# Attention, experts and a gated layer in one kernel: which queue loads the first batch's values of the strided heads

## The chip, the cores and the metric

The kernel runs on one core of one Trainium2 chip. The metric is the device time of one launch in microseconds (us). The engines are named as the profile names them: PE (TensorE, the matrix engine; PEld is its weight load), DVE (VectorE), ACT (ScalarE), POOL (GpSimd) and SP (SyncE). SP computes nothing here: its in-order queue issues nearly all transfers between HBM and the on-chip memory. POOL can issue transfers too, on a queue of its own, and computes besides.

## The reference, cut to what matters

Three stages follow one another; the output of one is the input of the next.

```python
# attention: 4 batches, 8 heads, 576 positions, head size 64
mask_local   = (rel >= 0) & (rel < 32)
mask_strided = (rel >= 0) & (pos[None, :] % 32 == pos[:, None] % 32)
masks = [mask_local for heads 0..3, mask_strided for heads 4..7]
scores = where(masks, q @ k.T / 8, -1e9);  attn = softmax(scores) @ v
# 2304 tokens x 512: noisy top-2 routing over 8 experts, relu(x @ w1) @ w2 each
# then rmsnorm, silu(xn @ w_gate) * (xn @ w_val) @ w_out
```

For a strided head, position `32*i + r` sees only the positions `32*i' + r` with `i' <= i`. So its scores fall apart into 32 residues `r` of 18 positions each, and the kernel treats six or seven residues together as one block of 108 or 126 rows.

## The kernel before, in words

The program is written out by hand in the order in which every engine is to run it; nothing reorders it afterwards. An engine's queue is in order, so an instruction that waits holds up all that stand behind it on that engine.

The attention is one loop over 40 units: for each batch `b` and kind (`"L"` local, heads 0 to 3; `"S"` strided, heads 4 to 7) five units `j`. The order is (0,L), (0,S), (1,S), (1,L), (2,S), (2,L), (3,S), (3,L). Pass `i` of the loop (lines 733 to 785) issues the scores of unit `i`, the transposes of the probabilities of unit `i-1`, the product with the values of unit `i-2` (`pv`, line 473) and the store of the result of unit `i-3` to the buffer `xd` in HBM (`store_x`, line 494). Beside its own scores a pass transposes queries and keys of the *next* group of units on PE (`t_unit`, line 336, whose transposes are line 344): during passes 3 and 4 those of (0,S), during passes 5 to 9 those of (1,S).

Three loaders feed this.

- `load_nat(b, kind)` (line 196, issue on line 205) brings queries and keys of four heads as they lie in HBM: eight loads of 128 positions each, key and query alternating (`natk`, `natq`), and two of the last 64 positions (`natr`). Every row that is moved is 256 bytes. All ten go through SP's queue.
- `load_vl(b)` (line 226) brings the values of the local heads in five loads through SP's queue.
- `load_vs(b, g)` (line 219, issue on line 222) brings the values of the strided heads for block `g` of residues (`vs0` to `vs4`), one load for each of four heads: 126 rows for the first two blocks, 108 for the other three, 256 bytes a row. These go through POOL's queue. For the first batch all twenty are issued at the start (lines 255 and 256); for later batches four at a time, in the loop, once `pv` has used the block before.

The program opens with the ten loads of (0,L), the five of the local values and the ten of (0,S) on SP (lines 238 to 240), while POOL sets constants and zero patches and then issues the twenty loads of `vs` for batch 0. On pass 3 `routing_consts` (line 312) adds three more loads to SP (`wgn` twice and `nz`) and some constants to POOL, and the first `store_x` follows. On pass 4 come the ten loads of (1,S).

The instructions that matter below are thus, on SP: line 205 (queries and keys), line 222 (strided values), lines 313, 314 and 316 (routing inputs), line 504 (results to `xd`); on PE: line 344 (transposes of queries and keys), line 480 (product with the strided values); on DVE: line 357 (the copy of the transposed strided keys to `ks`).

Of the kernel before, what the change touches and what calls it, by code (L numbers as in the profile page):

```python
# [24 lines left out]
def attn_moe_swiglu(ctx: ExitStack, tc: tile.TileContext, q, k, v, w_gate, w_noise, noise, w1, w2,  # L25
                    u_gate, u_val, u_out, rms_g, out):
    nc = tc.nc
    B, H, S, D = q.shape
# [18 lines left out]
    NI = S // WIN  # L47
# [148 lines left out]
    def load_nat(b, kind, parts=range(5)):  # L196

        h0 = 0 if kind == "L" else 4
        for a in parts:
            for nm, src in (("k", k), ("q", q)):  # L200
                n, o, m = (128, 0, 4) if a < 4 else (64, 0 if nm == "q" else 64, 1)
                key = (nm if a < 4 else "r", b, kind)
                if key not in nat:
                    nat[key] = ap_.tile([128, m, 256], F32, name="nat" + key[0], bufs=2)
                nc.sync.dma_start(nat[key][o:o + n, a % 4].rearrange("p (h d) -> p h d", d=D),
                                  bass.AP(tensor=src.tensor,
                                          offset=src.offset + ((b * H + h0) * S + a * 128) * D,
                                          ap=[[D, n], [S * D, 4], [1, D]]))

    vs_t = [ap_.tile([128, 4, D + 1], F32, name=f"vs{g}") for g in range(5)]  # L210
# [5 lines left out]
    qs2 = [[ap_.tile([128, S], F32, name=f"qs{i}{j}") for i in range(2)] for j in range(2)]  # L216
    ks2 = [[ap_.tile([128, S], F32, name=f"ks{i}{j}") for i in range(2)] for j in range(2)]

    def load_vs(b, g):
        r0, nr = GR[g]  # L220
        for h in range(4):
            nc.gpsimd.dma_start(vs_t[g][:nr * NI, h, 0:D],
                              bass.AP(tensor=v.tensor, offset=v.offset + ((b * H + 4 + h) * S + r0) * D,
                                      ap=[[D, nr], [WIN * D, NI], [1, D]]))

    def load_vl(b, parts=((0, 9),)):
        for t0, t1 in parts:
            if t0 == 0:
                nc.sync.dma_start(vl[32:96, 0, :, 0:D],
                                  bass.AP(tensor=v.tensor, offset=v.offset + b * H * S * D,  # L230
                                          ap=[[D, 64], [S * D, 4], [1, D]]))
                t0 = 1
            for h in range(4 if t1 > 1 else 0):
                nc.sync.dma_start(vl[:96, t0:t1, h, 0:D],
                                  bass.AP(tensor=v.tensor, offset=v.offset + ((b * H + h) * S + 64 * t0 - 32) * D,
                                          ap=[[D, 96], [64 * D, t1 - t0], [1, D]]))

    load_nat(0, "L", (0, 1, 2, 3, 4))
    load_vl(0)
    load_nat(0, "S")  # L240


    dif = ap_.tile([128, 128], F32, name="dif")
# [8 lines left out]
    nc.gpsimd.memset(vl[0:32, 0, :, 0:D], 0.0)  # L252
    for t in vs_t:
        nc.gpsimd.memset(t[:, :, D:D + 1], 1.0)
    for g in range(5):
        load_vs(0, g)
    identb = ap_.tile([128, 128], BF, name="identb")
    V.tensor_copy(identb, identf)
    mapf = ap_.tile([128, E * NT], F32, name="mapf")
# [473 lines left out]
    for i in range(NS + 3):  # L733
        u = subs[i] if i < NS else None
        if u:
            b, kd, j = u
# [25 lines left out]
        if 0 <= i - 2 < NS:  # L762
            w = subs[i - 2]
            pv(w)
            if w[0] + 1 < B:
                if w[1] == "S":
                    load_vs(w[0] + 1, w[2])
                elif w[2] == 4:
                    load_vl(w[0] + 1)
# [680 lines left out]
```

## Time and profile before

| what | value |
|---|---|
| median of 3 runs | 1095.3 us (1095.11 to 1097.02) |
| the profiled execution's own time | 1100.19 us |
| its span, first to last instruction | 1098.4 us |
| PE busy | 1051.4 us, 96% of the span |
| DVE, ACT, POOL busy | 700.1, 494.5, 223.1 us |
| moved by DMA | 196.13 MB, mean 179 GB/s |
| mean granted clock of TensorE | 0.982 of full |

The profile is of one execution, which took 0.4% longer than the median of the runs. Busy shares are averages over stages with different limits: the attention takes about the first 200 us and is a tightly coupled stage in which every engine waits for others, and the experts and the gated layer after it keep PE busy throughout. The stage of the change is the first 60 us.

### The profile page before, as it was taken

How to read it: one execution, taken by the hardware profiler on the slowest of the kernel's cores; microseconds unless marked ns; L12 is line 12 of the kernel's file. 1: busy time of each engine (PE TensorE's matmuls, PEld its weight loads, DVE VectorE, ACT ScalarE, POOL GpSimd, SP SyncE). 2: the span in 40 equal slices, each digit the busy share in tenths (PEclk: the TensorE clock that was granted, in tenths of full speed). 3: DMA queues.
4: the chain of work that ended last, by engine and by line, in shares of the span. 5: the costliest groups of instructions: out<-in, count | busy, mean ns of one | idle time of the engine just before them, and what ended most of it. 6: DMA issues, size and time to landing. Idle time of an engine off the chain costs nothing. (4 is left out here: it accounts for less than half of the span.)

```text
span 1098.4 us, 17694 instructions
## 1 busy us (share of the span) xinstructions
PE 1051.4 (96%) x6309; PEld 944.9 (86%) x6309; DVE 700.1 (64%) x1489; ACT 494.5 (45%) x1044; POOL 223.1 (20%) x261
## 2 busy tenths in 40 slices
PE   7988989999999999999999999999999999999998
PEld 5776777889989999999898989888999888999997
DVE  4666665457788788876354144878876566754554
ACT  4766652353443444443344144545454554543342
POOL 6565210303232323222200034111000220000000
PEclk8989889999999999999999999999999999999999
DMA  9977522358798898775444133455456554464431
GB/s 162 206 177 162 129 62 64 96 176 267 267 300 279 284 287 296 261 246 184 164 155 143 48 115 98 146 203 174 168 201 231 195 175 148 159 216 166 140 135 58
DMA packets 179418, 196.13 MB, mean 179 GB/s; under 512 B 66816, under 2 KB 135424, under 8 KB 179328
## 3 DMA queue, kind: packets, MB, share of 16 engines
q1 hardware_dynamic: 169264, 172.37, 49.8%
q0 software_dynamic: 9920, 22.35, 7.7%
q8 instruction: 50, 0.82, 0.3%
q14 instruction: 40, 0.33, 0.1%
q10 hardware_dynamic: 144, 0.26, 0.1%
HBM read 140.88 MB, written 54.00 MB: 177 GB/s over the span
## 5 line engine op out<-in xcount | busy, mean ns | idle before, releaser
L149 PE MATMUL bank<-xta,low 128*128 128x384 f32 x376 | 128.0, 340 | 3.1 <-DVE posu L956 2.0
L151 PE MATMUL bank<-xta,low 128*128 128x384 f32 x376 | 127.9, 340 | 0.0
L150 PE MATMUL bank<-xta,low 128*128 128x384 f32 x376 | 127.7, 340 | 0.0
L149 PE MATMUL bank<-ring,ha 128*128 128x512 f32 x288 | 114.3, 397 | 0.0
L150 PE MATMUL bank<-ring,ha 128*128 128x512 f32 x288 | 114.0, 396 | 0.0
L151 PE MATMUL bank<-ring,ha 128*128 128x512 f32 x288 | 114.0, 396 | 0.0
L149 PE MATMUL bank<-low 128*128 128x384 f32 x264 | 89.8, 340 | 7.3 <-ACT p L1294 7.2
L150 PE MATMUL bank<-low 128*128 128x384 f32 x264 | 89.7, 340 | 0.0
L151 PE MATMUL bank<-low 128*128 128x384 f32 x264 | 89.5, 339 | 0.0
L1030 POOL TENSOR_TENSOR dm<-dm,da 128x512 f32<-128x512 f32 x36 | 46.7, 1296 | 203.7 <-DVE da L1028 101.8
L162 ACT ACTIVATE ha<-bank 128x384 fp32r<-128x384 f32 x64 | 31.4, 490 | 116.5 <-PE bank L151 116.4
L149 PEld LDWEIGHTS bank<-xta,low 128*128 128x128 f32 x376 | 71.3, 190 | 11.4 <-issue 3.3
L163 DVE SCALAR_TENSOR_TENSOR ha<-bank,ha 128x384 fp32r<-128x384 f32 x64 | 35.4, 553 | 63.4 <-ACT ha L162 63.3
L150 PEld LDWEIGHTS bank<-xta,low 128*128 128x128 f32 x376 | 71.2, 189 | 4.9
L151 PEld LDWEIGHTS bank<-xta,low 128*128 128x128 f32 x376 | 71.2, 189 | 0.0
L846 POOL DMA_INDIRECT buf<-yd,posu x36 | 38.5, 1069 | 155.2 <-DMA yd<-buf 98.6
L1325 ACT ACTIVATE u<-u 128x384 f32<-128x384 f32 x32 | 16.8, 526 | 115.7 <-DVE u L1324 115.7
L151 PEld LDWEIGHTS bank<-ring,ha 128*128 128x128 f32 x288 | 54.0, 187 | 12.4 <-DVE ha L1127 0.3
L149 PEld LDWEIGHTS bank<-low 128*128 128x128 f32 x264 | 49.6, 188 | 15.7 <-ACT p L1294 9.8
L132 DVE TENSOR_TENSOR low<-stage,low 128x1024 fp32r<-128x1024 f32 x34 | 42.6, 1256 | 23.2 <-ACT low L131 21.4
L830 POOL DMA_INDIRECT buf<-xd,mapu x37 | 47.8, 1291 | 46.7 <-DVE posu L956 16.6
L149 PEld LDWEIGHTS bank<-ring,ha 128*128 128x128 f32 x288 | 54.1, 188 | 3.1 <-ACT ha L1125 0.3
(284 smaller groups left out, 2780.9 us busy)
## 6 DMA issues: line engine op xcount, KB each, us to landing
stage<-in_moe_w_dram SPq DMA_DIRECT2D x128, 256.0 KB
low<-ul SPq DMA_DIRECT2D x20, 896.0 KB
ul<-low SPq DMA_DIRECT2D x12, 896.0 KB
yd<-buf SPq DMA_DIRECT2D x40, 256.0 KB
ud<-dm SPq DMA_DIRECT2D x36, 256.0 KB
stage<-uc SPq DMA_DIRECT2D x16, 512.0 KB
wc<-uc SPq DMA_DIRECT2D x16, 512.0 KB
yd<-zero SPq DMA_DIRECT2D x28, 256.0 KB
```

What stands on the lines that cost most here:

```text
L132: lo_engine.tensor_tensor(r[:, 1], st, r[:, 0].bitcast(F32), op=OP.subtract)
L149: nc.tensor.matmul(o, l[(slice(None), 0) + lsl], r[(slice(None), 0) + rsl], start=first, stop=False)
L150: nc.tensor.matmul(o, l[(slice(None), 0) + lsl], r[(slice(None), 1) + rsl], start=False, stop=False)
L151: nc.tensor.matmul(o, l[(slice(None), 1) + lsl], r[(slice(None), 0) + rsl], start=False, stop=last)
L162: nc.scalar.activation(h[:, 0], p, AF.Relu)
L163: nc.vector.scalar_tensor_tensor(h[:, 1], p, 0.0, h[:, 0].bitcast(F32), op0=OP.max, op1=OP.subtract)
L830: nc.gpsimd.indirect_dma_start(t, None, xd, bass.IndirectOffsetOnAxis(ap=mapu[:, e * NT + j:e * NT + j + 1], axis=0))
L846: nc.gpsimd.indirect_dma_start(y, None, yd, bass.IndirectOffsetOnAxis(ap=posu[:, kk, t:t + 1], axis=0))
L1030: nc.gpsimd.tensor_tensor(m, m, a.bitcast(F32), op=OP.add)
L1325: nc.scalar.activation(u3, u3, AF.Silu)
```

## The change: which queue issues twenty loads, and where in it

`load_vs` gets the issuing engine as an argument. The twenty loads of batch 0 leave POOL's queue and stand in SP's queue behind the ten loads of the strided queries and keys. Later batches are loaded by POOL as before. What is loaded, the tiles, and every instruction of PE, DVE and ACT are the same.

```diff
-    def load_vs(b, g):
+    def load_vs(b, g, eng=nc.gpsimd):
         r0, nr = GR[g]
         for h in range(4):
-            nc.gpsimd.dma_start(vs_t[g][:nr * NI, h, 0:D],
+            eng.dma_start(vs_t[g][:nr * NI, h, 0:D],
                               bass.AP(tensor=v.tensor, offset=v.offset + ((b * H + 4 + h) * S + r0) * D,
                                       ap=[[D, nr], [WIN * D, NI], [1, D]]))
...
     load_nat(0, "L", (0, 1, 2, 3, 4))
     load_vl(0)
     load_nat(0, "S")
+    for g in range(5):
+        load_vs(0, g, nc.sync)
...
     for t in vs_t:
         nc.gpsimd.memset(t[:, :, D:D + 1], 1.0)
-    for g in range(5):
-        load_vs(0, g)
```

On SP's queue before, from the last load of (0,S) to the keys of (1,S) (`natk_413`; `xd` is the results' buffer, `x_340` the first unit's result):

```order
L205 DMA natr_159<-in_q_dram 64x4x64
L313 DMA wgn_217<-in_moe_w_gate_dram 128x4x8
L314 DMA wgn_217<-in_moe_w_noise_dram 128x4x8
L316 DMA nz_219<-in_moe_noise_dram 128x18x8
L504 DMA xd_62<-x_340 128x256
L205 DMA natk_413<-in_k_dram 128x4x64
```

And in the changed kernel, at the same place:

```order
L205 DMA natr<-in_q_dram 64x4x64
L222 DMA vs_115<-in_v_dram 126x1x64 x4
L222 DMA vs_116<-in_v_dram 126x1x64 x4
L222 DMA vs_117<-in_v_dram 108x1x64 x4
L222 DMA vs_118<-in_v_dram 108x1x64 x4
L222 DMA vs_119<-in_v_dram 108x1x64 x4
L313 DMA wgn<-in_moe_w_gate_dram 128x4x8
L314 DMA wgn<-in_moe_w_noise_dram 128x4x8
L316 DMA nz<-in_moe_noise_dram 128x18x8
L504 DMA xd<-x 128x256
L205 DMA natk<-in_k_dram 128x4x64
```

The twenty loads now stand between the keys and queries of (0,S) and everything that SP issued behind them: the routing inputs, the first result's store and the ten loads of (1,S).

On PE the order is unchanged. This is the piece of it in which the keys of (1,S) are first used; what PE does next, products and transposes of units that are already under way, stands behind them:

```order
L416 MATMUL bank0_101<-ks10_128,qs10_124 126x126
L470 MATMUL bank3_104<-identf_67,pp_437 96x128 x2
L344 MATMUL bank5_106<-identf_67,natk_413 128x128 x4
L484 MATMUL bank4_105<-vl_120,pts_431 64x65 x8
L515 MATMUL bank6_107<-identf_67,x_465 128x128 x2
```

These four transposes read all four 128-position loads of keys, the last of which is the seventh of the ten loads on SP. Nothing moved here.

## Rows read from the trace of the kernel before

**Rows 1.** The page: busy time of PE, and the granted clock in 40 slices

```profile
PE 1051.4 (96%) x6309; PEld 944.9 (86%) x6309; DVE 700.1 (64%) x1489; ACT 494.5 (45%) x1044; POOL 223.1 (20%) x261
PEclk8989889999999999999999999999999999999999
```

**Rows 2.** Timeline of PE: start us, us, engine, line, op, out<-in, count [idle before <-releaser]

```profile
3.24 0.66 PE L385 MATMUL bank<-identf,natk 128*128 128x128 f32 x2 [3.24 <-DMA natk<-in_k_dram]
...
21.86 0.48 PE L344 MATMUL bank<-identf,natk 128*128 128x128 f32 x1 [1.99 <-DMA natk<-in_k_dram]
22.12 1.06 PE L344 MATMUL bank<-identf,natq 128*128 128x128 f32 x4
23.11 1.14 PE L484 MATMUL bank<-vl,pts 96*64 96x65 f32 x16
...
31.34 0.60 PE L344 MATMUL bank<-identf,natk 128*128 128x128 f32 x4
31.88 0.69 PE L484 MATMUL bank<-vl,pts 96*64 96x65 f32 x16
...
37.59 0.99 PE L480 MATMUL bank<-vs,pts 126*126 126x65 f32 x8
```

**Rows 3.** Windows: stretch, its us, busy us of each engine (instructions), granted clock, DMA share, GB/s

```profile
9.64:19.20 9.56, 7.61 (x61) 6.50 (x60) 5.75 (x27) 6.77 (x24) 8.16 (x15) 1.00 1.33 181
16.88:21.86 4.98, 0.94 (x6) 0.33 (x4) 0.45 (x3) 2.38 (x9) 2.99 (x13) 0.99 1.34 186
21.86:28.90 7.04, 6.61 (x41) 5.66 (x41) 3.36 (x6) 2.97 (x6) 0.00 (x0) 0.52 1.03 139
...
31.30:45.80 14.50, 14.15 (x148) 11.88 (x147) 9.73 (x30) 11.37 (x34) 6.92 (x12) 1.00 0.97 197
```

**Rows 4.** Timeline of POOL: the twenty loads (two rows of four) and what follows

```profile
5.44 8.11 POOL L222 DMA_DIRECT2D vs<-in_v_dram  x13
...
17.35 1.80 POOL L222 DMA_DIRECT2D vs<-in_v_dram  x3 [0.40 <-DMA vs<-in_v_dram]
19.11 0.19 POOL L315 MEMSET wgn<- 128x64 f32 x1
```

**Rows 5.** DMA issues over all four batches: out<-in, queue, count, KB each

```profile
vs<-in_v_dram POOLq DMA_DIRECT2D x48, 27.0 KB
...
vs<-in_v_dram POOLq DMA_DIRECT2D x32, 31.5 KB
```

**Rows 6.** Timeline of SP's queue: start us, us of issue, line, out<-in, count

```profile
0.73 0.45 SPq L205 DMA_DIRECT2D natk<-in_k_dram  x1
...
9.64 1.20 SPq L205 DMA_DIRECT2D natk<-in_k_dram  x1
...
15.64 1.26 SPq L205 DMA_DIRECT2D natk<-in_k_dram  x1
...
18.59 0.61 SPq L205 DMA_DIRECT2D natr<-in_q_dram  x1
19.25 0.60 SPq L313 DMA_DIRECT2D wgn<-in_moe_w_gate_dram  x1
...
21.26 2.38 SPq L504 DMA_DIRECT2D xd<-x  x1
...
26.18 0.51 SPq L205 DMA_DIRECT2D natq<-in_q_dram  x1
...
27.83 0.51 SPq L205 DMA_DIRECT2D natk<-in_k_dram  x1
...
30.34 1.02 SPq L504 DMA_DIRECT2D xd<-x  x2
...
56.10 1.62 SPq L504 DMA_DIRECT2D xd<-x  x2
```

**Rows 7.** Waits of SP's queue in the first 60 us: who waited for whom, us, times, longest

```profile
SPq L504 <- DVE ks L357: 2.3, 1, 2.3
```

## The prediction

> **What bounds the kernel now.** The page comes first: PE is busy for 1051.4 of 1098.4 us, and the few slices with a lower granted clock lie in the first fifth [rows 1]. A change at the start therefore costs or gains what it moves PE's first stretch by; nothing behind it has idle time to take that up. Next the timeline of PE at the start: the last 128-position load of the strided keys of batch 0 arrives only at 21.86 us, and PE is held for it [rows 2]. [...] Third, SP's timeline: it issues without a pause, one transfer after the other, and the keys of (1,S), issued last at 27.83 us, are used by PE at 31.34 us without a wait but with little to spare [rows 2, 6]. [...]
>
> **What the change takes away.** POOL issues the twenty loads from 5.44 to 19.15 us [rows 4], beside SP's loads. Per batch they are 12 of 27.0 KB and 8 of 31.5 KB [rows 5], 576 KB or 0.59 MB; at the 181 to 186 GB/s of that stretch [rows 3] that is 3.2 us of the transfers' time. With them gone the last strided keys should land 3.2 us earlier, at 18.7 us, and SP, whose ten loads end at 18.59 + 0.61 = 19.20 us [rows 6], at 16.0 us. The bounds: nothing, if the second queue used time that SP's loads could not; and 4.1 us, if the ten loads, which took 9.64 to 19.20 us or 0.96 each, fell to the 0.55 of a quiet stretch (26.18 to 27.83 us, three steps) [rows 6]. I take 3.2, the one that follows from bytes. POOL is free 13.7 us earlier; the constants behind its loads [rows 4] hold nobody up, so that is worth nothing. The first wait of SP's queue also goes: the first store of a result stood from 21.26 us for 2.38 us, 2.3 of it behind the copy to `ks` on DVE [rows 6, 7], which follows those keys. In the new list SP arrives there long after that copy.
>
> **What it adds.** Twenty issues on SP, ahead of the routing inputs, the first store and the ten loads of (1,S). No row has this load on SP. The nearest have the same shape, residues by 18 positions, in the other direction: two stores of strided results take 1.62 us together, 0.81 each with the gap [rows 6]. The stores of local results, one row a partition, take 1.02 for two, 0.51 each, and the quiet loads 0.55 [rows 6]. So a load costs 0.55 to 0.81 us of SP's time and all twenty 11.0 to 16.2 us. I take 0.81, by the shape.
>
> [...]
>
> SP's list is then: 16.0, plus 16.2 for the twenty, is 32.2 us; the three routing inputs took 19.25 to 21.26 us, so 34.2; the store without its wait 0.6, so 34.8; the fourth load of keys of (1,S) is the seventh of its ten, 7 times 0.55, so 38.65 us. From the end of issue to use it was 2.1 us with empty queues (0.73 + 0.45 to 3.24 us), 5.0 in the crowded stretch (15.64 + 1.26 to 21.86), and at most 3.4 for these same keys before (28.34 to the fourth transpose at 31.7) [rows 2, 6]. With SP alone issuing I take 2.5: 41.1 us. PE's queue is in order, so all that stands behind these transposes, and with it ACT and DVE, waits. Before, the fourth transpose ran at 31.7 us: **9.4 us later**.
>
> **The clock.** PE would reach that place about 25 us (31.34 less the 3.2 and less the slow stretch's loss, below) and stand for some 15 us, three times the pause after which the clock fell before. So I count one slow stretch like that from 21.86 to 28.90 us behind it. Four transposes took 1.06 us there against 0.60 later, sixteen products 1.14 against 0.69 [rows 2]; at that ratio of about 0.6, 7.04 us lose **2.8 us**. The old slow stretch goes, but its gain only lengthens the new wait. Bounds: 0, if other work hides it, to 4.8, if it lasts 12 us.
>
> **What is hidden.** The values themselves land by about 34 us, and their first use, at 37.59 us before [rows 2], stands behind the stalled transposes, so they hold nobody. The next ten loads of SP, (1,L), and everything later move with SP by about as much as PE moves, so I expect no second stall and nothing given back.
>
> **Sum:** 9.4 + 2.8 = 12.2 us. The profiled execution's 1100.2 us would become 1112.4; the median of the runs, 4.9 us below it, 1095.3 + 12.2 = **1107.5 us**. A difference of 0.2% (2.2 us) is about what a measurement of this kernel can tell from no change.
>
> **The rivals.**
> - *The loads cost SP only what any load does*, 0.55 us. Then the twenty take 11.0 instead of 16.2, the stall shrinks by 5.2, and the sum is 7.0: 1102.3 us. For it: other shapes cost that. Against it: every strided store is dearer.
> - *Nothing is gained at the start.* If POOL's transfers ran in time that SP's could not use, the keys of (0,S) still land at 21.86 and SP's list starts at 19.2: 3.2 us more, 1110.7 us. The DMA share of 1.34 against 0.97 later [rows 3] speaks for a real queue and so against it.
> - *Not slower: the transfers, not SP's issuing, set when the keys land.* Then the moved bytes only change places. Last strided keys at 18.7; the rest of (0,S), 0.26 MB, until 20.1; the values' 3.2 until 23.3; routing inputs 2.0, store 0.6, seven loads 3.85 give 29.7 us instead of 31.7: 2.0 us faster, 1093.3 us. It decides where a load costs SP little: with p per load the keys land at 16.0 + 20p + 2.0 + 0.6 + 3.85 + 2.5, which is 31.7 at p = 0.34 us, below the shortest issue in these rows, 0.45. Against it also: 31.5 KB are 0.17 us of transfer at 186 GB/s, a fifth of the issue. [...]
>
> **How the numbers follow.** Forecast 0.62, cheap loads 0.20, no gain at the start 0.12, not slower 0.06. The range must reach down to the cheap loads (1102.3) and a part of the clock's loss less, 1100.5; up to no gain at the start with a landing slower by a microsecond, 1112.0. Left out are the not-slower case and the tails. Only that case is not slower by over 0.2%: its 2.0 us lie within the 2.2, so most of it counts as no change. Faster 0.02, the same 0.05, slower 0.93.
>
> **What would show it.** Right: no wait of PE for keys beyond some 19 us; twenty rows of line 222 on SP of about 0.8 us each from 16 to 32 us; a wait of PE on `natk` of some 15 us, ended near 41 us; a granted clock near 0.5 for about 7 us after it; the first product with `vs` near 49 us instead of 37.59; from there the same distances as before. Wrong: issues well under 0.5 us, a stall that ends before 32 us, or a first expert stage that starts when it did.

## The result, and the profile after

| | before | changed |
|---|---|---|
| median, us | 1095.67 (1095.11 to 1097.02, 4 runs) | 1108.47 (1107.86 to 1109.59, 4 runs) |
| ratio, with 95% interval | | 1.0103 (1.0084 to 1.0122) |
| the profiled execution: own time, span, us | 1100.19, 1098.4 | 1108.92, 1107.1 |

The change costs 12.8 us by the medians and 11.3 by the ratio (9.2 to 13.4); 12.2 were forecast. The page after: PE is busy for as long as before to within half a per cent [rows 1], in a longer span, and the second slice, 28 to 55 us, has a lower granted clock.

```profile
PE 1046.4 (95%) x6309; PEld 940.5 (85%) x6309; DVE 701.5 (63%) x1489; ACT 494.2 (45%) x1044; POOL 210.3 (19%) x241
...
PEclk9698889999999999999999999999999999999999
```

SP's timeline after (start us, us of issue, line, out<-in, count), beside [rows 6]:

```profile
16.02 0.62 SPq L205 DMA_DIRECT2D natr<-in_q_dram  x1
16.68 15.89 SPq L222 DMA_DIRECT2D vs<-in_v_dram  x20
32.62 0.46 SPq L313 DMA_DIRECT2D wgn<-in_moe_w_gate_dram  x1
...
34.29 1.14 SPq L504 DMA_DIRECT2D xd<-x  x1
35.53 0.38 SPq L205 DMA_DIRECT2D natk<-in_k_dram  x1
...
38.77 0.51 SPq L205 DMA_DIRECT2D natk<-in_k_dram  x1
```

The loads of (0,S) end at 16.64 us instead of 19.20; the twenty new ones take 0.79 us each, and the fourth keys of (1,S) are issued at 38.77 instead of 27.83. PE's timeline after, beside [rows 2]:

```profile
18.13 0.33 PE L344 MATMUL bank<-identf,natk 128*128 128x128 f32 x1 [0.88 <-DMA natk<-in_k_dram]
...
38.56 0.48 PE L344 MATMUL bank<-identf,natk 128*128 128x128 f32 x1 [12.91 <-DMA natk<-in_k_dram]
...
42.25 0.47 PE L344 MATMUL bank<-identf,natk 128*128 128x128 f32 x1 [0.80 <-DMA natk<-in_k_dram]
...
50.36 0.99 PE L480 MATMUL bank<-vs,pts 126*126 126x65 f32 x8
```

The strided keys of batch 0 are complete at 18.13 instead of 21.86 us: the start did gain. Then PE waits 12.91 us for the first keys of (1,S), and three times more for the others, to 42.25 us; before, the four ran from 31.34 us without a wait. (In a second profile of the kernel before, below, they ran from 31.62 us, and the fourth waited 0.26 us, to 32.37.) PE's waits for keys in the first 60 us, as the view of waits adds them up (us in total, times, longest), beside 3.1 us at the very start:

```profile
PE bank L344 <- DMA natk<-in_k_dram: 16.1, 5, 12.9
```

The windows after (columns as in [rows 3]) show the wait and what it leaves behind:

```profile
17.00:25.20 8.20, 6.26 (x73) 4.89 (x71) 4.72 (x13) 6.46 (x18) 0.00 (x0) 1.00 0.38 70
25.20:36.00 10.80, 0.45 (x4) 0.17 (x2) 0.75 (x2) 1.39 (x5) 0.00 (x0) 0.59 0.25 36
36.00:43.00 7.00, 2.18 (x10) 1.08 (x12) 0.17 (x1) 0.00 (x0) 0.00 (x0) 0.50 1.07 214
43.00:48.00 5.00, 5.00 (x41) 4.08 (x38) 2.35 (x6) 1.33 (x4) 0.00 (x0) 0.54 0.98 215
48.00:56.00 8.00, 8.00 (x83) 6.97 (x82) 5.25 (x16) 6.65 (x19) 4.81 (x8) 1.00 0.96 173
```

While SP issues the twenty, the DMA share is 0.38, then 0.25: the transfers are idle for most of the time in which everything waits for SP to issue. PE stands and the granted clock falls (0.59 from 25.2 to 36 us, 0.50 from 36 to 43); from 43 to 48 us PE is busy throughout at 0.54, and from 48 us on the clock is full again (1.00). What stands behind the four transposes on PE comes after them: the next products start at 42.66 us, DVE waits 16.8 us for the four to copy them to `ks`, and ACT 17.4 us for transposes behind them.

**From there nothing is given back.** Against a second profile of the kernel before (first experiment) the same instructions of DVE come 12.0 us later at 44 to 72 us, about 13 us later at 81 us, and 13.3 us later at the end. Against the first profile of before the shift is 12.8 us at 47 to 83 us and 8.8 at the end, since that execution lost some 4.5 us by itself later, 2.9 of them between 150 and 190 us.

### The profile page after: what moved, and what is told of

The parts are those of the page before. It is cut to its first block, busy times and chain, and to the rows that moved or that the text cites. A ratio compares the mean times of both kernels' runs of the same rounds, so it can differ in the third digit from the quotient of the medians.

```text
span 1107.1 us, 17694 instructions
## 1 busy us (share of the span) xinstructions
PE 1046.4 (95%) x6309; PEld 940.5 (85%) x6309; DVE 701.5 (63%) x1489; ACT 494.2 (45%) x1044; POOL 210.3 (19%) x241
## 5 line engine op out<-in xcount | busy, mean ns | idle before, releaser
L1325 ACT ACTIVATE u<-u 128x384 f32<-128x384 f32 x32 | 16.8, 526 | 115.8 <-DVE u L1324 115.8
```

The source lines that it names most:

```text
L1325: nc.scalar.activation(u3, u3, AF.Silu)
```

## The experiments

Each run is set against runs of the kernel before in the same comparison; their medians were 1096.34 us (first four experiments, 7 runs), 1099.66 (next four, 21 runs), 1097.18 (the three after them, 23 runs) and 1100.66 (the last, 3 runs). Absolute times are not compared between comparisons: the first four ran on one chip, the next four and the last on a second, the three between on a third. On the second chip the kernel before is some 3 us slower, and all five kernels profiled there fall 2.6 to 3.1 us further behind between 150 and 190 us; no profile of the other two chips changes by more than 0.4 us there. "Shift" is how much later the same instruction of DVE comes than in the second profile of the kernel before.

### The kernel before, once more

> The kernel before, unchanged, for a second profile of it. The two profiles so far differ by 12.8 us from 60 to 140 us but only by 8.8 us at the end, while the medians differ by 12.8 us. If the profiled execution of before lost about 4 us to itself around 160 to 185 us (its granted clock is 0.83 there), a second profile is some 4 us shorter (span near 1094 us) and runs parallel to the changed kernel at a distance of 12 to 13 us to the end. If the changed kernel really regains 4 us there, the second profile looks like the first (span near 1098 us).

One execution: 1095.62 us, span 1093.8, mean granted clock 0.989. The first profile was an execution 4.6 us longer. Up to 72 us the two lie within 0.8 us of each other; in the window 150 to 200 us the granted clock was 0.95 in the first and 0.99 in this one. So the 8.8 us that the change seems to cost at the end of the first pair of profiles are the full 12 to 13 us.

### What makes a load dear: two kinds of plain rows

Both kernels load rows that lie together in HBM, in place of residues by 18 positions; the first takes 128 rows for every load, the second as many rows as the real load.

```diff
+            if eng is nc.sync:
+                eng.dma_start(vs_t[g][:n, h, 0:D],
+                              bass.AP(tensor=v.tensor, offset=v.offset + ((b * H + 4 + h) * S + r0) * D,
+                                      ap=[[D, n], [1, D]]))    # n = 128, or nr * NI = 126 and 108
+                continue
```

> The changed kernel, but the twenty loads read 128 rows that lie together in HBM instead of residues by 18 positions, so the first batch's strided heads get other values than the reference's. Theory (SP's own time per load ahead of the keys of (1,S) sets the stall, and the shape makes it dear): a load costs 0.55 instead of 0.80 us, the block on SP 11 instead of 15.9 us, the fourth transpose of the keys of (1,S) runs near 37.3 instead of 42.25 us, the kernel is about 5 us faster than the changed one, near 1103.5 us. Rival (any load on SP costs the same): 1108.5 us. Rival (bytes set it): 1108.5 us, since no byte is saved.

> As the run with 128 plain rows, but 126 and 108 rows as in the changed kernel, still lying together, so again with other values. It tells the walk (7 or 6 by 18) from the number of rows. If the walk in three steps makes a load dear: 0.55 us each and near 1103.5 us, like 128 rows. If a row count that 16 engines cannot share evenly makes it dear: 0.75 us each and near 1108 us, like the changed kernel.

SP's timeline and PE's, 128 rows:

```profile
16.58 10.76 SPq L223 DMA_DIRECT2D vs<-in_v_dram  x20
```
```profile
36.96 0.47 PE L349 MATMUL bank<-identf,natk 128*128 128x128 f32 x1 [0.74 <-DMA natk<-in_k_dram]
...
45.27 0.99 PE L485 MATMUL bank<-vs,pts 126*126 126x65 f32 x8
```

And SP's timeline with 126 and 108 rows:

```profile
16.93 10.25 SPq L223 DMA_DIRECT2D vs<-in_v_dram  x20
```

The twenty issues one by one (shortest, median and longest in ns, first and last start in us), in the changed kernel, with 128 rows, and with 126 and 108:

```profile
L222 SPq DMA_DIRECT2D vs<-in_v_dram x20: 732/732/958, 16.7 to 31.8; - x20
```
```profile
L223 SPq DMA_DIRECT2D vs<-in_v_dram x20: 429/430/1512, 16.6 to 26.9; - x20
```
```profile
L223 SPq DMA_DIRECT2D vs<-in_v_dram x20: 340/372/1638, 16.9 to 26.8; - x20
```

128 rows: 1105.41 us (4 runs), ratio 1.0087 (1.0070 to 1.0103), 9.1 us slower. 126 and 108 rows: 1103.15 us (4 runs), ratio 1.0066 (1.0049 to 1.0083), 6.8 us slower. On average a load of plain rows takes 0.54 and 0.51 us of SP, one by residues and positions 0.79, with the same bytes in the second case. The averages of the plain rows contain one issue of 1.5 and 1.6 us that was held up by something the profile does not name; the usual issue took 0.43 us for 128 rows, 0.39 for 126 and 0.37 for 108, against 0.75 and 0.73 for 126 and 108 rows by residues. So it is not the odd number of rows that makes the issue dear but the pattern, 7 or 6 residues by 18 positions. The price reaches the end: the twenty issues are 5.1 us shorter with 128 rows, the fourth transpose comes 5.3 us earlier (36.96 against 42.25), the first product with the strided values 5.1 us earlier, and the shift at 43 to 63 us is 6.9 with 128 rows and 7.6 with 126, in place of 12.0. The gain over the changed kernel is 3.7 us with 128 rows and 6.0 with 126 by the medians, 1.8 and 4.1 by the ratios, with intervals some 4 us wide: in the total a gain is clear for 126 rows alone, and its size of some 5 us is read from the profiles.

### The dose: eight loads on SP, twelve on POOL

```diff
-    for g in range(5):
+    for g in range(2):
         load_vs(0, g, nc.sync)
...
+    for g in range(2, 5):
+        load_vs(0, g)
```

> Eight of the twenty loads (the first two blocks) on SP behind the keys and queries, the other twelve on POOL from the start as before. Theory (each load ahead of the keys of (1,S) costs SP 0.79 us): the block takes 6.3 instead of 15.9 us; the strided keys come 1.8 us later than in the changed kernel, because twelve loads still run beside them (0.33 MB at 184 GB/s); the fourth transpose of the keys of (1,S) runs near 42.25 - 9.5 + 1.8 = 34.5 us, 2.8 us later than before, the clock still falls: about 5 us slower than before, near 1101 us. Rival (a fixed price as soon as SP carries such loads): near 1108 us. Rival (only transfers count): not slower than before.

SP's timeline, then PE's:

```profile
19.90 6.57 SPq L222 DMA_DIRECT2D vs<-in_v_dram  x8
```
```profile
21.40 0.33 PE L346 MATMUL bank<-identf,natk 128*128 128x128 f32 x1 [0.89 <-DMA natr<-in_q_dram]
...
32.68 0.48 PE L346 MATMUL bank<-identf,natk 128*128 128x128 f32 x1 [2.69 <-DMA natk<-in_k_dram]
...
36.30 0.48 PE L346 MATMUL bank<-identf,natk 128*128 128x128 f32 x1 [0.76 <-DMA natk<-in_k_dram]
...
44.66 0.99 PE L482 MATMUL bank<-vs,pts 126*126 126x65 f32 x8
```

1107.05 us (4 runs) against 1099.66, ratio 1.0070 (1.0047 to 1.0093), 7.4 us slower: some 2 us more than expected. It is no fixed price that comes with the first such load: the keys below are 4.6 us late, with twenty loads 10.6. With twelve loads still on POOL the start gains only half a microsecond (21.40 against 21.86). SP's eight issues add 6.6 us ahead of the keys of (1,S); the first store behind them takes 1.2 us less than before, from its start to the next (it no longer waits [rows 7]), and the seven loads up to the fourth keys 0.9 less. The fourth transpose is 4.6 us later than in the first profile of before, 3.9 later than in the second. But the short stall brings the slow stretch too (the sixteen products behind the four transposes take 1.14 us, as in the changed kernel at a granted 0.50 to 0.54, against 0.69 at this place before [rows 2]): from the fourth transpose to the first product with the strided values 8.4 us, like the 8.1 after the long one (8.3 and 9.0 with the plain rows) and unlike the 5.9 before. **Here a clock that has fallen costs about the same behind a short wait as behind a long one** (2.69 and 12.91 us), which was missing from the expectation.

### The clock behind the stall: filling it

Extra transposes of a constant, whose results are overwritten, keep PE busy ahead of the four transposes: 78 and three times 6, then, since that left a gap, 118 and three times 8.

```diff
             for a in range(4):
+                if (b, kind, u) == (1, "S", 1):
+                    for _ in range(6 if a else 78):    # second kernel: 8 and 118
+                        nc.tensor.transpose(p[:, a * 128:(a + 1) * 128], identf, identf)
                 nc.tensor.transpose(p[:, a * 128:(a + 1) * 128],
```

> The changed kernel with 78 extra transposes of the identity on PE ahead of the first transpose of the keys of (1,S), and 6 ahead of each of the other three, into a bank that the real ones overwrite. They fill the stall and change no wait. Theory (the half clock after the stall is a term of its own, 2.8 us in the prediction): the clock stays at full, the rows behind the stall take 0.60 instead of 1.06 us, and the kernel is 2.3 to 2.8 us faster than the changed one, near 1106.0 us. Rival (the slow stretch is hidden by other waits): no change, 1108.5 us. If the fillers themselves delay PE, the stall's end moves and shows it.

PE's timeline with 78:

```profile
25.22 8.68 PE L346 MATMUL bank<-identf 128*128 128x128 f32 x78
...
38.84 0.47 PE L347 MATMUL bank<-identf,natk 128*128 128x128 f32 x1 [4.95 <-DMA natk<-in_k_dram]
...
43.37 0.34 PE L347 MATMUL bank<-identf,natk 128*128 128x128 f32 x1
...
49.35 0.99 PE L483 MATMUL bank<-vs,pts 126*126 126x65 f32 x8
```

1108.55 us (4 runs), ratio 1.0113 (1.0095 to 1.0132): nothing gained. The extra transposes ran out after 8.7 us, PE stood for 4.95 us and the clock fell (0.55 from 36 to 43 us); the sixes then ran at that clock and held up the real transposes by 1.1 us. Still the clock was back by then (0.95 from 43 to 48 us), and the first product came 1.0 us earlier than in the changed kernel. So this kernel does not show what the clock alone is worth, and the next one fills for longer.

> The changed kernel with 118 extra transposes of a constant on PE ahead of the first transpose of the keys of (1,S), and 8 ahead of each of the other three; what they write is overwritten. At 0.11 us each at full clock they should fill the wait from 25.2 us to the landing at 38.6 us, and most of the three steps of 1.2 us behind it. The list of SP and the landings are as in the changed kernel. Theory (the slow clock behind the stall is worth some 2.1 to 2.3 us, the stall itself is SP's list): the granted clock stays at 1.00 up to the fourth transpose, which comes at 42.3 us as in the changed kernel, the first product with the strided values at 48.2 instead of 50.4 us, and the ratio to the kernel before falls from 1.010 to about 1.008 (9 to 11 us slower than before). Rival (the clock is worth nothing, since DVE and ACT set that stretch): the first product stays near 50.4 us and the ratio at 1.010 or more.

PE's timeline with 118, and the windows 100 to 150 and 150 to 200 us:

```profile
25.21 13.04 PE L346 MATMUL bank<-identf 128*128 128x128 f32 x118
...
42.26 0.33 PE L347 MATMUL bank<-identf,natk 128*128 128x128 f32 x1
...
48.23 0.99 PE L483 MATMUL bank<-vs,pts 126*126 126x65 f32 x8
```
```profile
100.00:150.00 50.00, 42.81 (x432) 35.37 (x431) 33.38 (x125) 32.48 (x95) 21.41 (x24) 0.93 0.65 147
150.00:200.00 50.00, 44.03 (x378) 37.92 (x379) 30.31 (x143) 20.40 (x61) 3.05 (x3) 0.97 0.20 59
```

The profile is as the theory has it: full clock throughout (1.00 from 25 to 56 us), the fourth transpose where it was, the first product at 48.23 us instead of 50.36, shift 9.9 instead of 12.0. The stall itself does not move by being filled: it is SP's list. But the times do not follow: 1109.21 us (1104.63 to 1113.56, 6 runs), ratio 1.0116 (1.0092 to 1.0140). The profiled execution was the fastest of the six. The same kernel once more:

> The same kernel as in the run with 118 and 8 extra transposes, looked at once more, because its executions lay between 1104.6 and 1113.6 us with mean granted clocks between 0.986 and 0.994, and the profiled one was the fastest of them, with 0.994. Theory (the extra transposes do save the two microseconds behind the stall in every execution, and what the others lose, they lose at a later place by another fall of the clock): the first product with the strided values comes at 48.2 us again, and an execution of 1108 to 1112 us has a stretch after 60 us in which the granted clock is lower than in the other profile and PE takes 4 to 8 us longer. Rival (the extra transposes do not always hold the clock): in such an execution the granted clock falls before 50 us and the first product comes at 50 us or later.

```profile
48.42 0.99 PE L483 MATMUL bank<-vs,pts 126*126 126x65 f32 x8
```
```profile
100.00:150.00 50.00, 43.23 (x421) 35.96 (x418) 31.56 (x117) 32.20 (x92) 20.59 (x25) 0.90 0.66 147
150.00:200.00 50.00, 42.74 (x359) 36.16 (x359) 28.21 (x136) 20.87 (x66) 4.10 (x4) 0.90 0.21 61
```

This execution took 1114.46 us, 9.8 us more than the other. Up to 63 us the two agree to 0.5 us, the first product at 48.42; then this one falls behind, to 6.3 us between 115 and 190 us, where its granted clock is 0.90 in both windows against 0.93 and 0.97, and by another 3.5 us up to 560 us. From 120 to 130 us, where it loses 1.7 us, PE is busy for all 10 us at a granted clock of 0.63, against 7.96 us at 0.99 in the other. Not all of this belongs to the kernel: the execution ran on the second chip, on which the kernel before is 3.5 us slower (1100.66 against 1097.18), and some 3 us of the loss lie between 150 and 190 us, where every kernel profiled on that chip loses them. So **the slow stretch behind the stall is worth 2.1 us where it lies, and in the times they are not to be found**: the eight executions are 12.0 and 12.5 us slower than before in the medians, the changed kernel 12.8, and the six on one chip lie 8.9 us apart. Whether the filled kernel loses more there than the changed one, and why, is open.

### Behind the next keys instead of ahead of them

The twenty loads stay on SP but stand behind the ten of (1,S).

```diff
-    for g in range(5):
-        load_vs(0, g, nc.sync)
...
                 load_nat(*units[i // 5 + 2])
+                if i == 4:
+                    for g in range(5):
+                        load_vs(0, g, nc.sync)
```

> All twenty loads on SP, but behind the ten loads of (1,S) instead of ahead of them. Theory (SP's list has no room in its first 60 us, so 16 us of issue stall somebody wherever they stand): the keys of (1,S) arrive near 27 us and that stall goes, but what stands behind the loads now, the stores of the next results and the loads of (1,L), is 16 us late, the result buffers run out near 36 us, and PE is held until about 43 us: a later, shorter stall; 1095 to 1101 us. Rival (only the place ahead of the keys of (1,S) was wrong): about 4.5 us faster than before, near 1091 us.

SP's timeline, PE's and DVE's:

```profile
27.13 15.90 SPq L222 DMA_DIRECT2D vs<-in_v_dram  x20
43.14 0.87 SPq L502 DMA_DIRECT2D xd<-x  x2
```
```profile
28.26 0.33 PE L342 MATMUL bank<-identf,natk 128*128 128x128 f32 x1 [0.90 <-DMA natk<-in_k_dram]
...
45.68 1.68 PE L478 MATMUL bank<-vs,pts 108*108 108x65 f32 x8 [4.40 <-issue]
```
```profile
45.15 0.42 DVE L490 TENSOR_TENSOR x<-bank,rc 126x256 f32<-126x256 f32 x1 [5.24 <-DMA xd<-x]
...
58.40 0.42 DVE L490 TENSOR_TENSOR x<-bank,rc 108x256 f32<-108x256 f32 x1 [5.14 <-DMA xd<-x]
```

1108.81 us (4 runs) against 1099.66, ratio 1.0079 (1.0060 to 1.0099), 9.2 us slower: the mechanism was as expected, but not its size. The keys of (1,S) now come 3.4 us earlier than before and PE leads by 4.1 us at 30 us. Then DVE waits twice, 10.4 us in all, for a result buffer whose store stands on SP behind the twenty (the second time behind the ten loads of (1,L) and five of local values as well); PE's next product starts 0.11 us after DVE's copy ends. The shift goes from -4.1 us at 30 us to +10.1 at 74 us. The place of the loads in SP's list is thus not what costs: the 16 us are taken from whatever SP has to issue next.

### The gain at the start alone, without the cost on SP

The loads go back to POOL, which first copies one column of the last strided keys, so that they start only when those have landed (the copy is the one thing added). The second kernel also issues the keys and queries of (1,S) on pass 2 instead of pass 4.

```diff
+    gate = ap_.tile([128, 1], F32, name="gate")
+    nc.gpsimd.tensor_copy(gate, nat["k", 0, "S"][:, 3, 0:1])
     for g in range(5):
         load_vs(0, g)
...
-            if j == (4 if i < 5 else 1) and i // 5 + 2 < len(units):    # second kernel only
+            if j == (2 if i < 5 else 1) and i // 5 + 2 < len(units):
```

> The two halves of the change apart: the twenty loads stay on POOL's queue but start only when the last 128 strided keys have landed (a small copy on POOL reads them first). Theory (the later start is worth what the bytes beside the keys cost, and SP's issue is what the change lost): the strided keys land near 18 us as in the changed kernel, SP's list is as short as before, the keys of (1,S) land near 27 us instead of 31.7: about 4.5 us faster than before, near 1091 us. Rival (the gain at the start is swallowed by the next wait, or the loads now delay the keys of (1,S) as they delayed those of (0,S)): 1095 us, no change.

SP's first store and PE's transposes in the first of the two:

```profile
18.40 2.83 SPq L506 DMA_DIRECT2D xd<-x  x1
```
```profile
17.97 0.33 PE L346 MATMUL bank<-identf,natk 128*128 128x128 f32 x1 [0.79 <-DMA natk<-in_k_dram]
...
30.53 0.48 PE L346 MATMUL bank<-identf,natk 128*128 128x128 f32 x1 [1.57 <-DMA natk<-in_k_dram]
```

1101.40 us (11 runs), ratio 1.0011 (0.9998 to 1.0024): no change, where some 4.5 us faster was expected. The strided keys come at 17.97 us as in the changed kernel, 3.9 us earlier than before. But SP's first store stands for 2.83 us, up to 21.23 us, behind work of DVE (the view of waits names the reduction `nm`, line 443; the copy to `ks` ended at 19.46). The keys of (1,S) behind it land beside POOL's loads, the last at 30.53 us; PE, being early, waits for the last three of the four (1.26, 1.44 and 1.57 us), the sixteen products behind them take 1.14 us instead of 0.69, and by 44 us the shift is +0.45.

> As the run with POOL's loads later, and the ten loads of (1,S) stand on SP in pass 2 instead of pass 4, so ahead of the routing inputs and the first store, which waits for the copy of the strided keys. Theory (SP's order is the remaining bound there): the keys of (1,S) land by about 24 us, before PE wants them at 25, and the kernel is about 6.5 us faster than before, near 1089 us. Rival (the earlier loads only crowd those of (0,S) or something later holds PE): as without the move, near 1091 us.

In the second kernel, SP's store, PE's timeline and DVE's:

```profile
42.44 3.56 SPq L506 DMA_DIRECT2D xd<-x  x4
```
```profile
48.77 1.68 PE L482 MATMUL bank<-vs,pts 108*108 108x65 f32 x8 [4.97 <-issue]
```
```profile
48.25 0.42 DVE L494 TENSOR_TENSOR x<-bank,rc 108x256 f32<-108x256 f32 x1 [6.10 <-DMA xd<-x]
```

1101.32 us (11 runs), ratio 1.0016 (1.0006 to 1.0027), where some 6.5 us faster was expected. Now everything leads by 6.2 us up to some 41 us, and loses it at one place: DVE waits 6.1 us for a result buffer, whose store SP issues at 42.44 us behind the ten loads of (1,L) and five of local values.

### Clearing the next thing, and the next

From the second of those kernels: the five loads of batch 1's local values on pass 11 instead of pass 6; then also the ten of (1,L) on pass 8 instead of pass 6.

```diff
-                elif w[2] == 4:
+                elif w[2] == 4 and w[0]:
                     load_vl(w[0] + 1)
+        if i == 11:
+            load_vl(1)
...
-            if j == (2 if i < 5 else 1) and i // 5 + 2 < len(units):    # second kernel only
+            if j == (2 if i < 5 else 3 if i < 10 else 1) and i // 5 + 2 < len(units):
```

> The kernel with POOL's loads held until the strided keys have landed and the loads of (1,S) two passes sooner, and besides the five loads of the second batch's local values on pass 11 instead of pass 6. In that kernel without this last edit PE was 6 us ahead at 43 us and lost it at 48 us, where DVE waited 6.1 us for a result buffer whose store stood on SP behind ten loads of (1,L) and these five. Theory (whatever SP is late with next takes back what was gained before): the five loads took 37.55 to 42.34 us, so the stores are issued some 4.8 us sooner, the wait of DVE on the result buffer shrinks from 6.1 to 1 to 2 us, and the kernel is 3 to 5 us faster than the one before, if no store or load after that stands late. Rival (SP's list is full all the way up to some 90 us, so the loss only moves to the next store or load): no change, within 1.5 us of the kernel before.

> As the run before, and the ten loads of queries and keys of (1,L) on pass 8 instead of pass 6, behind two more stores of results; they are first used on pass 10. Theory (SP's list bounds the first 60 us and only its order can be chosen): the stores of the first results come another 5 us sooner on SP, no wait of DVE on a result buffer is left in the first 60 us, but the keys of (1,L) land some 5 us later, close to their first use; 4 to 6 us faster than the kernel before if that still suffices. Rival: PE now waits for the keys of (1,L), and the gain over the run before is nothing or negative.

In the first, SP's store, ACT's and PE's timeline, and the window 61 to 72 us; last, that window in the second profile of the kernel before:

```profile
36.89 3.02 SPq L506 DMA_DIRECT2D xd<-x  x4
```
```profile
61.97 1.04 ACT L131 CAST low<-stage 128x1024 fp32r<-128x1024 f32 x1 [2.59 <-DMA stage<-in_moe_w_dram]
```
```profile
63.73 1.14 PE L472 MATMUL bank<-identf,pp 128*96 128x128 f32 x4 [2.33 <-ACT pp L456]
```
```profile
61.00:72.00 11.00, 8.68 (x69) 7.79 (x68) 5.44 (x26) 7.12 (x19) 7.10 (x9) 0.69 0.97 214
```
```profile
61.00:72.00 11.00, 10.18 (x109) 9.46 (x111) 9.05 (x47) 9.15 (x28) 7.91 (x11) 1.00 0.82 210
```

1098.30 us and 1098.27 us (12 runs each) against 1097.18; ratios 1.0010 (0.9999 to 1.0022) and 1.0008 (0.9997 to 1.0019). Neither is faster than the kernel before. The stores do come 5.6 us sooner (36.89 against 42.44), DVE's wait is gone, and PE leads by 6.2 us up to 62 us. There ACT waits 2.59 us to convert expert weights that are still under way; the probabilities stand behind that on ACT and come at 63.33 us, PE waits 2.33 us for them, and the granted clock of the window is 0.69 against 1.00. By 81 us the lead is gone (shift +0.4). In the second kernel the lead of 5.5 us at 62 us is a shift of +2.7 at 84 us. There ACT waits 4.3 us for the weights; PE waits for the keys of (1,L) for 0.4 us, so the rival of that run named the wrong late item. The rival of the first is right: the loss moves to the next thing that is late. The trace points at SP's list more than at the transfers, whose share is 0.97 against 0.82: SP issues the last of these weights at 56.73 us, only 2.0 us sooner than in the second profile of before (58.70) though PE leads by 6.2, and from issue to landing they take 5.2 us, not more than the 5.6 of before. Whether crowded transfers slowed SP's earlier issues is not told apart. No version here beats the kernel before.

## Why the prediction was right

**The mechanism held at each step.** Strided keys: forecast 18.7 us, measured 18.13. Twenty issues on SP of about 0.8 us: measured 0.79. One long wait of PE for the keys of (1,S), a slow stretch behind it, no second stall, and nothing given back: all as forecast.

**The sizes.** The fourth keys of (1,S) were forecast for 41.1 us and came at 42.25. Term by term, in SP's list: the end of (0,S) 16.64 for 16.0 (+0.6); the twenty 15.98 from end to next start for 16.2 (-0.2); the routing inputs 1.67 for 2.0 (-0.3); the first store 1.24 for 0.6 (+0.6), with no wait left in it that the profile names, so the store by itself was put too low; the seven loads 3.75 for 3.85 (-0.1); from the end of issue to use 2.97 for 2.5 (+0.5). Against the 31.7 us of before the stall is 10.6 us where 9.4 were forecast. The clock was over-sized by a little: 2.2 us by the distance from the fourth transpose to the first product (8.1 against 5.9 us), 2.1 us by filling the stall, where 2.8 were forecast from the slow stretch in [rows 2, 3]. So part of the closeness is luck: the errors of +1.2 and -0.6 us partly cancel, as do those within SP's list. The sum of 10.6 + 2.2 = 12.8 us equals the medians to a tenth by luck too: against the second profile of before it is 9.9 + 2.1 = 12.0.

**The rivals.** *Cheap loads*: fell, and the plain rows show why it was a rival. Twenty loads of plain rows, 126 and 108, do cost 0.51 us each on average, so the shape alone made the forecast; with the cheap pattern the kernel was 6.8 to 9.1 us slower, near the 7.0 of that rival. *Nothing gained at the start*: fell by the 18.13 us; with the loads held back on POOL the strided keys come as early (17.97). *Not slower, since the transfers set the pace*: fell. Plain rows of the same bytes also made the stall 5 us shorter. Here 15.9 us of issue moved what 3.2 us of transfers could (the prediction's estimate from 576 KB and the 181 to 186 GB/s of [rows 3]), with the DMA share at 0.25 to 0.38.

**A reason that is not shown.** The runs show the dear issue by its pattern alone: 0.75 and 0.73 us for 7 and 6 residues by 18 positions, 0.39 and 0.37 for as many rows that lie together. The trace of the changed kernel has 8 and 7 semaphore events behind these loads of 126 and 108 rows, and 16 behind each load of queries and keys; whether that has to do with the price, or the two-level walk itself nearly doubles it, no run here tells apart. The forecast's 0.81 us rested on the strided stores [rows 6] and holds without the reason.

## What to carry to other kernels

Where one in-order queue issues nearly all transfers, ask of a load moved onto it what the *issue* costs, by a row of the same access pattern, and what stands behind it. Here bytes and DMA share did not tell it (the share was 0.25 to 0.38 while SP issued): 20 issues of 0.8 us pushed back everything in the list, and placing them later only changed who waited: keys, result buffers or weights. For the same reason a lead of six microseconds that a kernel wins early was worth nothing here while the list that feeds it stayed as long, so look at the whole list, not at its first late item.

## What the runs showed of the hardware that was not expected

- The same 31.5 KB and 27.0 KB cost SP 0.75 and 0.73 us of issue as 7 or 6 residues by 18 positions, and 0.39 and 0.37 us as rows that lie together (0.79 and 0.51 us a load on average, with gaps and held-up issues).
- A wait of 2.69 us and three shorter ones lengthened the stretch behind them by as much (8.4 us in place of 5.9) as a wait of 12.91 us did (8.1).
- Six executions of one kernel on one chip lay 8.9 us apart (23 of the kernel before 5.9), and 2.1 us saved at 48 us were not to be found in the total. Two profiles of that kernel that agree to 0.5 us up to 63 us end 9.8 us apart; some 3 us of that is the chip, on which five kernels lost 2.6 to 3.1 us at the same place.
